# A new order for a fused attention and feed-forward kernel: in-place squares, one ring of eleven tiles, and the last stores in parts

## The chip, the cores and the metric

The kernel runs on one core of a Trainium2 chip. The metric is the device time of one execution in microseconds. The core has five engines that each work through their own list of instructions in order: TensorE (PE, with its weight loads as PEld), VectorE (DVE), ScalarE (ACT), GpSimd (POOL) and SyncE (SP), which here only issues DMAs. An instruction that waits holds up everything behind it on its engine.

## The reference

An attention with a squared relu in place of the softmax, and then a feed-forward block with a quick gelu. There are 8 batches, 12 heads, 448 positions, 64 elements a head; 3584 tokens, 768 model columns and 2048 inner columns.

```python
scores = scale * np.matmul(q, k.transpose(0, 1, 3, 2))
attn = np.maximum(scores, 0.0) ** 2 / S
x = np.matmul(attn, v)          # then the heads side by side: [3584, 768]
h = x @ w_in
g = h * (1.0 / (1.0 + np.exp(-1.702 * h)))
out = g @ w_out
```

The scale and the division by S are left for later in the kernel: the gelu's input and the last copy carry a factor 1/SC.

## The kernel before

**The attention** is cut into 24 units, one for four heads of one batch (three units a batch). A unit has seven blocks j of 64 rows. `scores` (line 150) makes a block's scores with four quarter-array matmuls (64 rows by 64 columns of the array each, side by side) into two PSUM banks. `relu` takes one bank to half of a float16 tile, on VectorE (line 161) or ScalarE (line 163). `square` (line 88 or 169) squares the whole tile on one of three engines into a tile of the pool `at`. `attn_v` (line 182) then multiplies the unit's seven tiles with v, again in quarter-array matmuls, into two banks, and `xt_evac` copies these into the transposed input of the feed-forward block. A relu tile comes from one of three pools `rl0` to `rl2` with one tile each, named by a number in the list; `at` has eight tiles. A square frees the relu tile, attn_v frees the `at` tiles.

**The loads.** k and q come either through GpSimd's queue, which casts them on the way (units 1 to 5, then transposed on TensorE, line 131), or through SP as float32 (`Lk`, `Lq`), are cast on an engine (`K`, `Q`) and are transposed by a DMA from SP (`Rk`, `Rq`, line 119). v comes through GpSimd's queue (`V`, line 104), and so do the weights w_in (eight DMAs, `jwa` and `jwb`, two for each of four blocks) and w_out.

**The feed-forward block** works on eight groups g of 384 and 512 tokens in turn. The first group and part of the second use plain matmuls (`m1`, line 229: `f` in the list). The others use a scheme with seven products of half-size blocks instead of eight (`unit_product`, `u`; sums of blocks are made on VectorE, `S`, `T`, `W`, `A`). Copies out of PSUM (`t`), sums (`b`), the gelu on ScalarE (`g`, line 215) and a widening on GpSimd (`v`, line 218) follow. The second matmul does the same with pairs of token tiles m (`pair_product`, `p`; `h` and `l` take the results to a float32 tile `osb`), and `store` (`o`, line 329) sends each tile out in two DMAs of 64 rows on SP. All full-array matmuls but those of `m1` are recorded at line 204, all two-operand elementwise work at line 88.

**The order** is written out by hand in one long list of words. Each word issues the instructions of one step, in the list's order, to the engine that its suffix names (`:a`, `:d`, `:p`; without one, a home engine), and `@` gives PSUM banks. Every engine thus gets its instructions in the list's order, and between engines only data and free buffers decide. For example `s6.1@0.2 r6.1.1:d@1 x6.1:a` is scores of block 1 of unit 6 into banks 0 and 2, a relu on VectorE into relu pool 1, and the square on ScalarE. Ten matmuls on zeros stand before the list.

Of the kernel before, what the change touches and what calls it, by code (L numbers as in the profile page):

```python
# [9 lines left out]
F16 = mybir.dt.float16  # L10
AF = mybir.ActivationFunctionType
# [4 lines left out]
def kernel(  # L16
# [35 lines left out]
    for name, bufs in (("cst", 1), ("kst", 1), ("qst", 1), ("k16", 2), ("q16", 2), ("v16", 4),  # L52
                       ("kT", 3), ("qT", 3), ("rl0", 1), ("rl1", 1), ("rl2", 1), ("at", 8), ("xe", 1), ("xo", 2),
                       ("T1", 1), ("T2", 1), ("T4", 1), ("ge", 1), ("go", 1), ("gf", 5),
                       ("as0", 1), ("as1", 1), ("osb", 3)):
        pool(name, bufs)
# [97 lines left out]
    rls = {}  # L154

    def relu(e, p, u, j, a):
        if (u, j) not in rls:
            rls[u, j] = new(f"rl{p.pop(0)}", [128, 2, S], F16, "rl")
        o, i = rls[u, j][:, a, :], slots[u, j][a][:, 0:S]
        if e == "d":  # L160
            nc.vector.tensor_scalar(out=o, in0=i, scalar1=0.0, scalar2=None, op0=ALU.max)  # L161
        else:
            nc.scalar.activation(out=o, in_=i, func=AF.Relu)  # L163

    def square(e, p, u, j):
        rl = rls.pop((u, j))
        at = new("at", [128, 2, S], F16)
        if e == "a":
            nc.scalar.activation(out=at, in_=rl, func=AF.Square)  # L169
        else:  # L170
            tt(at, rl, rl, ALU.mult, e)
        slots[u, j] = at
# [157 lines left out]

    def m2(e, p, g, m, h):
        op[g, m, h] = bank(p, "op")
        mm(op[g, m, h][:, 0:NOUT], lambda f: gts[g][:, f, m * 128:(m + 1) * 128],
           lambda f: wout[h][f // WO][:, f % WO, :], NF, True)
# [82 lines left out]
    with tc.manual_schedule():  # L417
# [3 lines left out]
               "l": pair_last, "i": single, "n": m2_out, "jo": load_w_out, "a": attn_v,  # L421
# [27 lines left out]
        zero = new("gf", [128, 1024], F16, "zero")  # L449
        nc.vector.memset(zero[:, 0:512], 0.0)  # L450
        zp = bank([7], "zp")
        for _ in range(10):
            nc.tensor.matmul(out=zp, lhsT=zero[:, 0:128], rhs=zero[:, 0:512],  # L453
                             start=True, stop=True)
        words = (
            "I Lk0 K0:d tk0@0 jk1 Lq0 Q0:a jq1 V1 V0 ek0 tq0@1 jk2 tk1@2 eq0 s0.1@3.4 s0.0@5.6 "
            "ek1 r0.1.1@0 s0.3@7.0 r0.1.0:d r0.3.1@1 tq1@1 r0.3.0:d s0.4@2.4 r0.0.0@2 s0.5@3.0 "
            "x0.1 x0.3 s0.2@7.5 r0.0.1 x0.0 r0.4.0@0 r0.4.1 s0.6@6.2 r0.5.0:d@1 x0.4 r0.6.1@2 eq1 "
            "jq2 tk2@4 s1.0@3.2 r0.5.1 r0.6.0 x0.6 r0.2.1@0 x0.5 r0.2.0 x0.2 ek2 r1.0.0@2 r1.0.1 "
            "x1.0 s1.1@0.6 r1.1.1@1 s1.2@1.5 tq2@7 eq2 r1.2.1:d@0 jwa1 jq3 r1.2.0 jk4 jk3 r1.1.0 "  # L460
            "s1.3@3.2 a0@6.4 jwa0 jwb0 r1.3.1@2 s1.4@1.0 r1.3.0 e0.0.1:a jwb1 x1.3 e0.1.1 jq4 "
            "x1.2:a tq3@7 s1.6@2.5 r1.6.1@2 s2.0@3.4 eq3 e0.0.0 V2 s1.5@7.5 r1.6.0 e0.1.0 "
            "s2.2@6.2 jwa3 r1.4.0:d@0 x1.1:p x1.6 jwb3 r1.4.1 x1.4 tk3@1 ek3 r1.5.1@1 r1.5.0 "
            "r2.0.0@2 tk4@0 r2.0.1 x1.5 s2.3@5.7 r2.3.1@0 s2.1@3.1 r2.3.0 V3 r2.2.0@1 ek4 x2.0 "
            "r2.2.1 r2.1.0@2 a1@4.7 r2.1.1:d x2.3 e1.0.0 s2.5@5.0 r2.5.1:d@0 jq5 e1.0.1:a e1.1.1 "
            "x2.2:a x2.1:p jk5 s2.4@6.2 f0.0.0@1 f0.2.0@3 r2.5.0 f0.2.1 f0.0.1 e1.1.0 s2.6@0.7 "
            "x2.5 s3.0@5.4 r2.4.1@1 f0.3.0@2 r2.4.0 r2.6.0@2 r2.6.1 f0.3.1 jwa2 r3.0.0:d@0 x2.4 "
            "f0.1.0@6 s3.1@0.5 r3.0.1 r3.1.1@1 f0.4.0@7 G3 Lk6 f0.1.1 x2.6 a2@4.5 r3.1.0:d x3.0:p "
            "tq4@0 S1.1 e2.0.0 x3.1 f0.4.1 e2.0.1:a f0.2.2 f0.3.2 e2.1.1 g0.2 jwb2 g0.3 f0.1.2 "
            "e2.1.0:a g0.1 eq4 f0.0.2 s3.4@5.3 s3.3@0.2 r3.4.0:d@2 g0.0 f0.5.0@4 r3.4.1 r3.3.0@0 "  # L470
            "V4 f0.4.2 f0.5.1 g0.4 v0.4 s3.2@6.1 r3.2.1@1 r3.2.0 r3.3.1:d x3.4 x3.3 s3.5@5.3 "
            "s3.6@2.0 f0.5.2 f0.6.0@7 f0.6.1 r3.6.1:d@2 r3.6.0 Lq6 r3.5.0@0 f0.7.0@1 x3.2 r3.5.1 "
            "x3.6 tk5@6 s4.1@0.2 g0.5 s4.0@5.3 r4.1.0@1 v0.1 jo0.1 f0.7.1 f0.7.2 v0.3 f0.6.2 "
            "r4.0.0@2 x3.5 r4.0.1:d ek5 r4.1.1 g0.6 x4.0 v0.5 s4.3@4.0 s4.2@5.3 S0.1 a3@2.6 "
            "r4.3.0@0 s4.4@7.4 g0.7 V5 r4.2.1@2 r4.2.0:d r4.3.1:d tq5@1 e3.0.0:a x4.3 x4.1 "
            "e3.0.1:a x4.2 S0.2 s4.6@3.5 r4.4.0@0 s4.5@0.2 f0.9.0@6 f0.9.1 r4.6.1@1 f0.9.2 eq5 "
            "r4.5.0:d@2 f0.12.0@7 f0.8.0@5 f0.12.1 f0.12.2 r4.6.0:d r4.4.1 f0.10.0@4 f0.10.1 v0.7 "
            "f0.10.2 v0.0 x4.6 r4.5.1 s5.3@2.1 g0.12 g0.9 s5.0@0.7 jo1.0 x4.4:p g0.10 r5.0.0@0 "
            "s5.2@3.6 r5.2.1@1 r5.0.1 x5.0:a f0.8.1 f0.8.2 x4.5 v0.10 r5.3.1:d@2 a4@4.0 e4.0.0:a "
            "s5.6@1.6 v0.12 f0.15.0@7 f0.15.1 f0.15.2 g0.8 r5.3.0:d r5.2.0:d r5.6.1@0 v0.9 S1.2 "  # L480
            "x5.3 r5.6.0:d s5.4@2.3 e4.0.1 s5.1@4.5 g0.15 x5.6:a s5.5@1.6 r5.1.0@2 r5.1.1:d "
            "f0.13.0@0 f0.13.1 f0.13.2 S2.1 S2.2 x5.2:a jo0.0 f0.14.0@7 r5.5.0@0 v0.8 x5.1:p "
            "f0.11.0@5 f0.14.1 f0.14.2 f0.11.1 Q6:d jo1.1 f0.11.2 r5.5.1:d r5.4.1:d@1 r5.4.0 "
            "f1.1.0@4 g0.13 x5.4 f1.5.0@1 v0.2 v0.6 v0.15 f1.1.1 x5.5 f1.5.1 K6:p S2.3 g0.11 "
            "f1.3.0@2 f1.2.0@0 a5@5.6 g0.14 Lk7 e5.0.0:a f1.6.0@3 f1.6.1 f1.0.0@7 e5.0.1:a f1.5.2 "
            "g1.5 S2.4 f1.4.0@5 S3.1 T1.1 T1.2 S3.2 W0.1 v0.14 v0.13 v1.5 f1.4.1 u1.3.0@6 t1.3.0 "
            "f1.1.2 S3.4 Rq6 v0.11 T1.4 g1.1 K7 f1.3.1 f1.4.2 f1.3.2 f1.2.1 f1.2.2 V6 W1.1 W1.2 "
            "W3.1 f1.0.1 f1.0.2 g1.0 u1.2.0@1 t1.2.0 Lq7 u1.3.1@4 v1.1 u1.2.1@7 g1.4 v1.0 b1.2.1 "
            "u1.3.2 Q7:a m0.0.0@5 f1.6.2 g1.2 Rk6 v1.2 b1.3.1 S1.4 W2.1 S0.3 S3.3 Lq8 g1.3 V7 Lk8 "
            "g1.6 Rk7 u1.2.3 v1.4 v1.6 n0.0.0 Rq7 s6.1@0.2 W3.2 s6.0@5.3 r6.0.1@2 W2.2 Q8 "  # L490
            "r6.0.0:d u1.3.3 r6.1.1:d@1 r6.1.0:d u1.2.2 s6.2@3.5 K8:p f1.7.0@2 g1.3.1 v1.3.1 "
            "x6.0:a g1.2.1 r6.2.1:d@0 f1.7.1 f1.7.2 v1.2.1 r6.2.0:d T1.3 t1.3.2 W2.4 t1.2.2 "
            "m0.0.1@0 g1.7 x6.1:a u1.2.4 S1.3 x6.2 s6.4@5.3 n0.0.1:a r6.4.0@2 s6.3@2.0 v1.7 W0.2 "
            "Lq9 t1.2.4:d b1.2.3 v1.3 Rq8 r6.4.1 x6.4 r6.3.1@1 r6.3.0 u1.3.4 t1.3.4:d u1.2.5 "
            "g1.2.5 u1.2.6 Q9 s6.5@5.3 r6.5.1:d@0 s6.6@0.2 x6.3:a b1.2.6 b1.3.3 r6.6.0@2 r6.6.1 "
            "x6.6:a g1.2.6 v1.2.6 m0.1.0@1 Lk9 s7.1@3.0 Rk8 Lq10 s7.0@7.2 r6.5.0:d x6.5 n0.1.0:a "
            "r7.1.0:d@1 r7.0.1@2 K9:p r7.1.1:d r7.0.0 g1.3.3 u1.3.6 b1.3.6 u1.3.5 x7.0 s7.2@5.1 "
            "W3.4 s7.3@3.2 v1.2.5 g1.3.5 r7.2.0@0 r7.2.1 g1.3.6 a6@0.7 g1.2.3 v1.2.3 v1.3.5 "
            "e6.0.1:a s7.4@4.6 r7.3.1:d@2 Lk10 K10:p x7.1 s7.5@5.1 x7.2:a m0.1.1@2 Q10:d e6.0.0 "
            "V11 e6.1.0:a e6.1.1:a r7.4.0@1 r7.3.0:d v1.3.6 r7.4.1 Rq9 r7.5.1@0 r7.5.0:d x7.5:a "  # L500
            "x7.3 x7.4 Rk9 s7.6@0.7 s8.1@3.4 n0.1.1:a r7.6.1@2 s8.0@5.6 r8.0.0:d@1 r7.6.0:d x7.6 "
            "m0.2.0@1 Lq11 r8.1.1:d@0 s8.2@5.2 s8.3@0.7 r8.1.0 o0.1 a7@3.4 r8.0.1 x8.0 r8.3.0@2 "
            "r8.3.1 v1.3.3 A1.0.1@0 r8.2.1@1 V8 V10 Lk11 r8.2.0:d x8.1:a s8.4@6.0 e7.0.0 x8.3 "
            "e7.1.0:a r8.4.0@0 s8.5@7.5 e7.0.1:a Q11 r8.5.0@2 x8.2 A1.0.2@1 r8.4.1 e7.1.1:a "
            "r8.5.1:d x8.5 n0.2.0:a m0.2.1@2 s8.6@3.6 s9.1@7.5 Rk10 r8.6.1@1 x8.4 r9.1.1@2 "
            "s9.0@0.4 r9.0.1@0 p1.0.0@1 n0.2.1:a h1.0.0 r9.0.0 Lq12 s9.3@6.5 r8.6.0:d x8.6 "
            "r9.3.0@1 Rq10 r9.1.0:d W0.3 a8@3.4 s9.2@2.7 r9.3.1 x9.1:a s9.4@0.6 e8.0.1:a K11:d "
            "e8.0.0 W1.3 x9.0 p1.0.2 r9.4.1@2 u2.1.0@5 r9.2.0@0 T2.1 Q12 t2.1.0 T2.2 W1.4 e8.1.1 "
            "u2.0.0@6 u2.1.1@2 b2.1.1 W2.3 T2.3 r9.2.1:d e8.1.0:a t2.0.0 r9.4.0 x9.4:a u2.1.2 "
            "u2.0.2 u2.2.0@3 t2.0.2 u2.0.1@4 g2.1.1 Rq11 t2.1.2 b2.0.1 u2.2.1@0 v2.1.1 g2.0.1 "  # L510
# [154 lines left out]
```

## Time and profile before

| | us |
|---|---|
| median of 13 runs | 373.16 (370.46 to 379.81) |
| profiled execution, device time | 371.45 |
| its span in the trace | 369.7 |
| PE, DVE, ACT, POOL busy | 358.5, 300.6, 269.3, 172.6 |
| mean granted TensorE clock | 0.994 |
| first matmul starts, last one ends | 1.2, 364.1 |

The three ways of squaring a tile take 660 ns on VectorE (97 of them), 952 on ScalarE (49) and 1755 on GpSimd (22); a relu takes 617 ns on VectorE (117) and 555 on ScalarE (219). A group's mean is the time from start to end of one instruction; neighbours on an engine overlap a little, so that a sum of means is some 10% above the busy time. Instructions named `ox` and `hx` are the products of the feed-forward block, `sc` the scores, `av` attn_v.

### The profile page before, as it was taken

How to read it: one execution, taken by the hardware profiler on the slowest of the kernel's cores; microseconds unless marked ns; L12 is line 12 of the kernel's file. 1: busy time of each engine (PE TensorE's matmuls, PEld its weight loads, DVE VectorE, ACT ScalarE, POOL GpSimd, SP SyncE). 2: the span in 40 equal slices, each digit the busy share in tenths (PEclk: the TensorE clock that was granted, in tenths of full speed). 3: DMA queues.
4: the chain of work that ended last, by engine and by line, in shares of the span. 5: the costliest groups of instructions: out<-in, count | busy, mean ns of one | idle time of the engine just before them, and what ended most of it. 6: DMA issues, size and time to landing. Idle time of an engine off the chain costs nothing.

```text
span 369.7 us, 9188 instructions
## 1 busy us (share of the span) xinstructions
PE 358.5 (97%) x3566; PEld 232.5 (63%) x3566; DVE 300.6 (81%) x532; ACT 269.3 (73%) x536; POOL 172.6 (47%) x222
## 2 busy tenths in 40 slices
PE   8899999999899999999999999999999999999993
PEld 4445555655488556875589555885549855688651
DVE  4899999899998887979989888887799689455741
ACT  3897874789798999867777868779978765566311
POOL 6776776736327336475436633146332634115300
PEclk9899999999999999999999999999999999999999
DMA  9999999997995596486953663849073440401224
GB/s 193 189 205 214 237 170 204 200 223 152 190 253 94 122 219 131 111 179 143 189 113 103 140 147 75 181 123 164 12 230 76 70 91 4 111 0 45 78 52 129
DMA packets 64908, 51.39 MB, mean 139 GB/s; under 512 B 35680, under 2 KB 61280, under 8 KB 64864
## 3 DMA queue, kind: packets, MB, share of 16 engines
q1 hardware_dynamic: 48256, 36.71, 42.6%
q0 software_dynamic: 16608, 14.09, 26.5%
q8 instruction: 28, 0.46, 0.5%
q14 instruction: 16, 0.13, 0.1%
HBM read 45.61 MB, written 11.01 MB: 153 GB/s over the span
## 4 chain that ended last, share of the span: by engine, by line
PE 77%; DVE 10%; DMA 4%; issue 3%; ACT 3%; POOL 1%; SPq 0%; DVEq 0%; ACTq 0%; POOLq 0%
PE ox L204 26%; PE hx L204 22%; PE av L182 8%; PE sc L150 7%; PE ht L229 5%; PE os L204 4%; PE op L204 3%; DVE at L88 3%; DVE rl L161 3%; DVE gf L88 2%; DMA q<-in_q_dram 2%; DMA v<-in_v_dram 1%; PE zp L453 1%; DMA out_dram<-osb 1%; ACT rl L163 1%
## 5 line engine op out<-in xcount | busy, mean ns | idle before, releaser
L163 ACT ACTIVATE rl<-sc 128x448 f16<-128x448 f32 x219 | 106.9, 555 | 18.8 <-PE sc L150 13.8
L161 DVE TENSOR_SCALAR rl<-sc 128x448 f16<-128x448 f32 x117 | 69.1, 617 | 8.3 <-PE sc L150 6.9
L218 POOL TENSOR_SCALAR go<-gf 128x512 f16<-128x512 f32 x64 | 43.1, 674 | 62.3 <-ACT gf L215 50.8
L88 DVE TENSOR_TENSOR at<-rl 128x896 f16<-128x896 f16 x97 | 61.8, 660 | 2.3 <-ACT rl L163 0.9
L88 POOL TENSOR_TENSOR at<-rl 128x896 f16<-128x896 f16 x22 | 38.5, 1755 | 50.1 <-ACT rl L163 22.9
L204 PEld LDWEIGHTS <-win 128*128 128x128 f16 x624 | 56.8, 98 | 6.8 <-issue 1.0
L88 DVE TENSOR_TENSOR gf<-hx,gf 128x512 f32<-128x512 f32 (+1 forms) x78 | 47.4, 625 | 15.8 <-PE hx L204 8.3
L218 POOL TENSOR_SCALAR ge<-gf 128x384 f16<-128x384 f32 x64 | 36.6, 572 | 34.6 <-ACT gf L215 31.0
L150 PE MATMUL sc<-qT,kT 64*64 64x448 f16 x672 | 49.9, 359 | 2.3 <-DVE qT L83 1.0
L215 ACT ACTIVATE gf<-gf 128x512 f32<-128x512 f32 (+1 forms) x78 | 43.5, 577 | 7.5 <-DVE gf L88 7.2
L169 ACT ACTIVATE at<-rl 128x896 f16<-128x896 f16 x49 | 46.3, 952 | 2.3 <-DVE rl L161 1.7
L204 PE MATMUL ox<-wout,go 128*128 128x384 f16 x256 | 46.0, 327 | 0.1
L204 PEld LDWEIGHTS <-winS 128*128 128x128 f16 x468 | 42.7, 98 | 5.2 <-issue 1.4
L204 PEld LDWEIGHTS <-go 128*128 128x128 f16 x320 | 30.0, 98 | 24.0 <-issue 5.5
L79 ACT ACTIVATE gf<-hx 128x512 f32<-128x512 f32 (+1 forms) x54 | 28.8, 546 | 16.7 <-PE hx L204 13.7
L204 PEld LDWEIGHTS <-ge 128*128 128x128 f16 x288 | 26.9, 98 | 21.5 <-issue 5.0
L182 PE MATMUL av<-at,v 64*64 64x448 f16 x672 | 37.9, 357 | 0.5 <-DMA v<-in_v_dram 0.4
L204 PE MATMUL hx<-T,winS 128*128 128x256 f16 (+1 forms) x312 | 36.0, 260 | 0.2
L150 PEld LDWEIGHTS <-kT 64*64 64x64 f16 x672 | 18.0, 105 | 24.5 <-issue 18.4
L204 PE MATMUL ox<-wT,asum 128*128 128x384 f16 x176 | 31.6, 327 | 0.0
L204 PE MATMUL hx<-xo,win 128*128 128x256 f16 x252 | 31.4, 273 | 0.1
L182 PEld LDWEIGHTS <-v 64*64 64x64 f16 x672 | 20.9, 109 | 13.6 <-issue 3.6
(78 smaller groups left out, 479.9 us busy)
## 6 DMA issues: line engine op xcount, KB each, us to landing
out_dram<-osb SPq DMA_DIRECT2D x56, 192.0 KB, 3.2
kst<-in_k_dram SPq DMA_DIRECT2D x19, 448.0 KB, 4.7
qst<-in_q_dram SPq DMA_DIRECT2D x19, 448.0 KB, 4.4
v<-in_v_dram POOLq DMA_DIRECT2D x24, 224.0 KB, 6.1
win<-in_moe_w_in_dram POOLq DMA_DIRECT2D x8, 384.0 KB, 10.9
wout<-in_moe_w_out_dram POOLq DMA_DIRECT2D x4, 768.0 KB, 10.3
k<-in_k_dram POOLq DMA_DIRECT2D x5, 224.0 KB, 7.0
q<-in_q_dram POOLq DMA_DIRECT2D x5, 224.0 KB, 7.6
```

The source lines that it names most:

```text
L79: nc.scalar.activation(out=o, in_=i, func=AF.Copy)
L88: eng[e].tensor_tensor(out=o, in0=x, in1=y, op=op)
L150: nc.tensor.matmul(out=sc[a][c, 0:S], lhsT=st["kT"][r, j, c], rhs=st["qT"][r, :, c], start=True, stop=True)
L161: nc.vector.tensor_scalar(out=o, in0=i, scalar1=0.0, scalar2=None, op0=ALU.max)
L163: nc.scalar.activation(out=o, in_=i, func=AF.Relu)
L169: nc.scalar.activation(out=at, in_=rl, func=AF.Square)
L182: nc.tensor.matmul(out=av[s][64 * a:64 * a + 64, 0:S], lhsT=v16[r, a, 64 * j:64 * j + 64], rhs=at[r, a, :], start=(j == 0), stop=(j == J - 1))
L204: nc.tensor.matmul(out=o, lhsT=lhs(i), rhs=rhs(i), start=start and i == 0, stop=i == n - 1, skip_group_check=True)
L215: nc.scalar.activation(out=o, in_=i, func=AF.Gelu_apprx_sigmoid, scale=1.0 / SC)
L218: eng[e].tensor_scalar(out=o, in0=i, scalar1=SC, scalar2=1.0, op0=ALU.mult, op1=ALU.mult)
L229: nc.tensor.matmul(out=hp[g, f][:, 0:n], lhsT=w[:, i, fo:fo + 128], rhs=xts[g][:, i, 0:n], start=i == 0, stop=i == NK - 1)
L453: nc.tensor.matmul(out=zp, lhsT=zero[:, 0:128], rhs=zero[:, 0:512], start=True, stop=True)
```

## The change

The list is a new one. It has the same steps for the same data with 1939 words against 1931, and differs in four ways beside its order.

```diff
-                       ("kT", 3), ("qT", 3), ("rl0", 1), ("rl1", 1), ("rl2", 1), ("at", 8), ("xe", 1), ("xo", 2),
+                       ("kT", 3), ("qT", 3), ("at", 11), ("xe", 1), ("xo", 2),
...
-        if (u, j) not in rls:
-            rls[u, j] = new(f"rl{p.pop(0)}", [128, 2, S], F16, "rl")
+        if (u, j) not in ats:
+            ats[u, j] = new("at", [128, 2, S], F16)
...
     def square(e, p, u, j):
-        rl = rls.pop((u, j))
-        at = new("at", [128, 2, S], F16)
+        at = ats.pop((u, j))
+        slots[u, j] = at
         if e == "a":
-            nc.scalar.activation(out=at, in_=rl, func=AF.Square)
+            nc.scalar.activation(out=at, in_=at, func=AF.Square)
         else:
-            tt(at, rl, rl, ALU.mult, e)
-        slots[u, j] = at
+            tt(at, at, at, ALU.mult, e)
...
+    def store_part(e, p, g, m, h, i):
+        b, j = divmod(gcum[g] + 2 * m + i, J)
+        r0 = b * S + j
+        c = slice(h * NOUT, (h + 1) * NOUT)
+        (nc.scalar if e == "a" else nc.sync).dma_start(
+            out=out[r0:r0 + 63 * J + 1:J, c], in_=osb[g, m][64 * i:64 * i + 64, c])
...
-        zero = new("gf", [128, 1024], F16, "zero")
-        nc.vector.memset(zero[:, 0:512], 0.0)
-        zp = bank([7], "zp")
-        for _ in range(10):
-            nc.tensor.matmul(out=zp, lhsT=zero[:, 0:128], rhs=zero[:, 0:512],
-                             start=True, stop=True)
+        zero = wT[2][:, 0, :]
+        nc.vector.memset(zero, 0.0)
+        zp = []
+
+        def zeros(e, p, n):
+            if p:
+                zp.append(bank(p, "zp"))
+            for _ in range(n):
+                nc.tensor.matmul(out=zp[0][:, 0:NOUT], lhsT=zero[:, 0:128], rhs=zero,
+                                 start=True, stop=True)
+
+        two["z"] = zeros
         words = (
-            "I Lk0 K0:d tk0@0 jk1 Lq0 Q0:a jq1 V1 V0 ek0 tq0@1 jk2 tk1@2 eq0 s0.1@3.4 s0.0@5.6 "
...
+            "Lk0 z13@0 jk1 V1 jq1 I V0 K0:d tk0@1 z1 ek0 jk2 Lq0 Q0:a tq0@2 eq0 tk1@3 s0.3@4.5 "
...
-            "l7.2.1 p7.2.2 A7.2.4 o7.1 p7.2.3 h7.2.2 p7.2.4 p7.0.6 l7.0.6 o7.0 h7.2.4 l7.2.3 "
-            "p7.2.5 l7.2.5:a o7.3 p7.2.6 l7.2.6 o7.2"
+            "q7.2.0.0:a p7.2.3 h7.2.2:d A7.2.4 p7.2.4 o7.1 p7.0.6 h7.2.4:d l7.2.3 l7.0.6 o7.0 "
+            "q7.3.1.1:a q7.2.0.1 q7.3.1.0:a p7.2.5 l7.2.5:a q7.3.0.0 q7.3.0.1 p7.2.6 l7.2.6 "
+            "q7.2.1.1:a q7.2.1.0"
```

The relu writes into the tile that the square then overwrites, so one pool of eleven tiles takes the place of three relu pools and eight tiles. The last two output tiles (7, 2 and 7, 3) go out as eight parts of 64 rows by 384 columns, four on ScalarE's queue and four on SP's, instead of four of 64 rows by 768 columns on SP's. The matmuls on zeros are 14 of 384 columns instead of ten of 512, 13 ahead and one after the first transposes, on a piece of a weight tile. The identity for the transposes is made by GpSimd after its first three loads instead of before them.

How many steps each engine gets, in the two lists:

| step | before: VectorE, ScalarE, GpSimd | after |
|---|---|---|
| relu | 117, 219, 0 | 121, 215, 0 |
| square | 97, 49, 22 | 84, 57, 27 |
| cast of k and q | 10, 8, 20 | 2, 14, 22 |
| copies of half-size products (`t`, `h`) | 37, 74, 0 | 40, 71, 0 |
| last sums and copies (`l`, `n`) | 40, 16, 0 | 41, 15, 0 |

The other steps keep their engines and numbers: 40 of the copies out of attn_v on ScalarE and 32 on VectorE, all gelus on ScalarE, all widenings on GpSimd.

## The prediction

> **What bounds the kernel now.** I read the page's busy times first, then the slices, the stage table, the chain that ended last in order of time, and last the stores at the end.
>
> ```profile
> span 369.7 us, 9188 instructions
> PE 358.5 (97%) x3566; PEld 232.5 (63%) x3566; DVE 300.6 (81%) x532; ACT 269.3 (73%) x536; POOL 172.6 (47%) x222
> PE   8899999999899999999999999999999999999993
> PEclk9899999999999999999999999999999999999999
> ```
>
> TensorE is busy 97% of the span; the next engine, VectorE, 81%. The only weak slices of PE are the first two and the last.
>
> ```profile
> 6.00:16.90 10.90, 9.05 (x146) 5.43 (x144) 10.20 (x19) 8.44 (x19) 7.59 (x11) 0.84 1.22 190
> 30.00:60.00 30.00, 29.84 (x311) 15.76 (x308) 28.67 (x48) 23.32 (x50) 20.42 (x27) 1.00 1.21 211
> 60.00:100.00 40.00, 38.88 (x347) 22.52 (x344) 37.95 (x63) 31.25 (x62) 21.57 (x27) 1.00 1.09 192
> 160.00:260.00 100.00, 99.59 (x1016) 67.52 (x1013) 83.81 (x151) 77.48 (x151) 48.97 (x61) 1.00 0.66 139
> ```
>
> The columns are stretch, length, then PE, PEld, DVE, ACT, POOL busy (with counts), granted clock, DMA share and GB/s. Up to 100 us VectorE is as full as PE (37.95 of 40); later it has 16% to spare. The clock is below 1 only before 17 us.
>
> Busy PE includes matmuls that crawl, so I set the starts of the 3566 matmuls in the timeline against what each kind takes back to back. That comes from the chain: 16 of 384 columns in 2.60 us, six of 256 in 0.64 to 0.66, 28 of attn_v in 1.32. The matmuls without the ten on zeros add up to 325 us. The first matmul starts at 1.2, the last ends at 364.1, so 38 us are something else: 1.2 before the first; 4.3 for the zeros; 12.2 for 111 changes between quarter-array (64x64) and full-array matmuls (below); about 9 for the small steps between groups and the transposes' latency; and about 12 of real waiting beyond each step's median, split into some 5 before 20 us, 1.1 from 20 to 30, and 5.7 from 30 to 364. After the last matmul come 5.6 us. So what an order can still win is small: about ten microseconds inside, two or so at the end.
>
> **The change part by part.**
>
> **In-place squares and one ring: nothing.** There are as many tiles as before (3 and 8 against 11). VectorE's in-place subtraction on go (1024 columns) averages 704 ns, the one from go into asum 776, so in-place costs nothing extra. The ring lets a relu start wherever any tile is free instead of one of three; its worth is in the waits below.
>
> **What moves between engines.** Counted in the two lists, at the page's means. VectorE: 13 squares fewer (x 660 ns, -8.6), eight casts of k and q fewer (4 x 0.65 + 4 x 1.09, -6.9), four relus, three copies out of PSUM, two last sums more and one copy fewer (+5.0): -10.5 us. ScalarE: eight squares (x 952, +7.6) and six casts (+5.7) more, four relus and some copies fewer (-4.3): +9.0. GpSimd: five squares (x 1755) and two casts more: +10.8. With 81, 73 and 47% busy all of it lies beside PE; the cover of VectorE grows just where it was full, up to 100 us. The matmuls are the same ones, and 14 on zeros of 384 columns replace 10 of 512, 5376 columns against 5120; both finish about when k's first cast does (it ends at 4.99), so 0.
>
> **Changes of array mode: +1.3 us.** Here a rule speaks against the change.
>
> ```profile
> 127.60 0.50 PE sc L150 x8
> 128.11 1.41 PE ox L204 x8
> ...
> 201.16 1.30 PE ox L204 x8
> 202.46 1.49 PE hx L204 x18
> ```
>
> Eight ox matmuls between scores hold PE for 1.41 us; between hx products, which are full-array too, 1.30. One change costs 0.11 us; the median over all of them is 0.105 one way and 0.113 the other. The Trainium skill (TensorEngine Tiling (Array Packing), Key Properties) says that changing the tiling mode drains TensorE, but gives no price. In the new list the modes change 138 times against 126, since ten scores stand alone between full-array groups where two did. By the row, 12 x 0.11 = +1.3 us; by the rule, more than nothing. I take the row.
>
> **The start: -0.5 us.** The first load on GpSimd's queue is issued at 1.45 behind the identity; in the new list it comes first, some 0.7 earlier. The loads then land one behind another, 1.1 us apart (k1 6.95, q1 8.11, v1 9.22, v0 10.33, k2 11.46), and PE waits for k2 (11.46, its transposes start at 11.51) and q2 (13.75, at 13.79). Half to all of 0.7 comes through: -0.5. The w_in parts now come in another order. At 1.95 us each behind 1.1 us per k, q or v I get the pairs at about 23, 28, 30 and 40 us, in the order w_in blocks 0, 1, 2, 3; PE wants them at about 25, 32, 33 and 45 (list position plus the 9.6 us by which PE lags its work at 24 us). They are hidden with 2 us left at the least; if that cover is gone, each us late is one us. Bounds -1.5 to +1.5.
>
> **Waits inside: -2.5 us of 5.7.** Two show in the chain.
>
> ```profile
> 94.64 1.20 issue
> 95.84 0.62 DVE rl L161
> 96.46 0.04 issue
> 96.50 0.38 PE sc L150 x3
> ...
> 251.22 5.46 DMA v<-in_v_dram
> 256.73 1.52 PE av L182 x28
> ```
>
> At 95.3 PE waits 1.4 us for a bank that VectorE's relu still holds. At 256 it waits 0.55 for v of unit 18, which GpSimd issued at 251.22, behind widenings. The new list has that load some 60 us of matmul work ahead of its product instead of 4.5, so the 0.55 goes. The other 5.1 are this kind of late reader of a bank, mostly 0.1 to 0.3 each. For every bank that is taken again I added up the matmul work between its last product and the next: under 1.5 us in 32 places before (smallest 0.64) and in 13 in the new list (smallest 1.17), past 25 us. In proportion 5.1 would become 2.1; not every wait is of this kind, so I take -2.0, with 0.55 -2.5. Bounds: -4.5, and 0.
>
> **Late k, q and v: +0.2 us.** The other side of the same list. Matmul work between the later cast of k or q and the unit's first scores: before, 14 us or more from unit 7 to 23; now 7.7 for unit 7, 9.9 for 8, 10.4 for 9, 9.7 and 9.4 for 22 and 23. A cast on GpSimd (1.0 us) and a DMA transpose from issue to landing (7.4 to 8.1 us for units 7 and 8, 3.0 to 5.0 for the late ones) need 9 together around 70 us, and 6 late. SP is in order too: behind a transpose that waits for its cast stand the next loads of k and q and then the stores. Before products, the v of unit 8 has 5.1 us of matmul work and that of unit 6 6.3, against 6.1 median (7.2 to 7.7 there) to land. If GpSimd works exactly at its place in the list, unit 7 is 1.4 late, v of unit 6 0.9, v of unit 8 2.3, unit 9 some 0.5: 5 us is the upper bound, 0 the lower. In the trace of before six such transfers land within 2 us of their use (v of units 2, 8, 14, 18, 23, k of unit 6), and only one made PE wait, 0.55 in all, since an in-order engine that is half idle runs a few us ahead of its place. Six tight ones again: 0.1 each would be 0.5; I take +0.2 because the start now arrives earlier.
>
> **The end: -0.5 us.**
>
> ```profile
> 364.08 0.02 issue
> 364.10 0.56 DVE osb L390
> ...
> 363.00:368.00 5.00, 1.07 (x7) 0.42 (x5) 0.56 (x1) 0.29 (x1) 0.00 (x0) 1.00 0.81 236
> ```
>
> After the last sum (364.66) SP issues two stores of 192 KB one behind the other (median 0.53 each), and the last lands 2.6 us after its issue, at 367.7; the DMA is busy all that time with three tiles (1.18 MB at 236 GB/s). Now only half a tile is left, in two parts of 96 KB, one issued by ScalarE and one by SP; that tile's other half goes before. The Trainium skill (DMA: Bandwidth & Descriptors, Issuing engines are not separate DMA queues) says that issuing from several engines saves only issue time, since all share 16 DMA engines. By it and by the row one issue is saved, 0.5; by half the bytes at 236 GB/s another 0.8 at most, if the backlog sets the end. The latency of 2.6 stays either way, so I take -0.5 (0 to -1.3). ScalarE's DMA issues aren't shown in this trace: at SP's 0.47 to 1.42 two stand ahead of its copy of the second last product, which comes 1.6 us after them; covered up to 0.8 each.
>
> **Sum.** +1.3 - 0.5 - 2.5 + 0.2 - 0.5 = -2.0 us. The profiled execution took 371.45 (span 369.7 and 1.75 around it), so it would take 369.4. The median of the runs, 373.16, stands 0.46% above that execution; 369.4 x 1.0046 = 371.1.
>
> **The rivals.**
>
> *The waits don't shrink (372.8 us).* PE is full already, and some of the 5.7 is the unevenness of the matmuls' own starts, which no order removes. For: outside 95 and 256 us no wait is above 0.3. Against: 32 tight banks become 13. With 0.8 instead of 2.5 and half a us more for late transfers: -2.0 + 1.7 = -0.3, so 372.8.
>
> *Late transposes and v (376 us, slower).* One mechanism, at units 6 to 9, 65 to 105 us: the casts and loads moved towards their use. There DMA is full (share 1.09 in the stage table), VectorE too, and a late kT lets PE run through what full-array work stands in the list and then stop. Price: up to the 5 us above, with -2.0 - 0.2 = -2.2 elsewhere +2.8, so 371.45 + 2.8 times 1.0046 = 375.5; with a cold clock or a second missed bank after it 376 and more. It decides from 3.5 us of such waits on. For: lists of 7.7 us against 9 needed. Against: before, five of six tight transfers cost nothing.
>
> *VectorE or ScalarE becomes the bound.* ScalarE gets 9 us more, 278 of 369, and from unit 0 to 5 it has 40.7 us of back-to-back work against 45.7 of PE's. That is below PE in every stage; I give it no chance of its own.
>
> **How the numbers follow.** Within 0.5% (1.9 us, about what a measurement of this kernel can tell from no change) means 371.3 to 375.0. The likeliest case, 371.1, has 0.50, its own range 368.5 to 372.3; I see 0.42 of it below 371.3. No gain: 0.26, of it 0.03 faster, 0.20 same, 0.03 slower. Late transfers: 0.24, of it 0.21 slower. So faster 0.45, same 0.31, slower 0.24. The range for 8 in 10 goes from the low bounds of waits and end (-4.5 and -1.3, against +1.3: 367.5) to the slow rival, 376.0.
>
> **What would show it.** Right: PE's last matmul ends at 361.5 to 363; no single wait of PE above 1 us past 30 us; VectorE below 292 us busy, ScalarE near 276; the last landing 3.2 us after the last matmul instead of 3.7. Wrong: PE idle before scores with the transposes of units 7 to 9 as releaser, or before attn_v of units 6 or 8 with v's DMA; PE waiting for w_in at 24 to 46 us; or the same end of PE with the same small waits. I would be most wrong if a late unit 7 delayed relus, squares and widenings behind it as well.

## The result, and the profile after

| | before | after |
|---|---|---|
| median of the runs, us | 373.39 (48 runs, 370.46 to 379.81) | 369.21 (11 runs, 368.68 to 371.75) |
| ratio of the times | | 0.9898 (95% interval 0.9870 to 0.9925) |
| profiled execution, device time and span | 371.45, 369.7 | 371.75, 369.9 |
| PE, DVE, ACT, POOL busy | 358.5, 300.6, 269.3, 172.6 | 358.2, 289.0, 276.6, 178.5 |

The kernel became 1.0% faster, 4.2 us between the medians; 2.0 were forecast. The ratio and its interval leave out a few runs of before that fell into a slower state, so the ratio is not quite the quotient of the two medians.

The two profiled executions are the wrong pair to compare. That of before is one of its better ones (371.45 against a median of 373.4); that of after is the slowest of its eleven. A common execution of the new order is at hand from the experiment `e4_tail_balanced` below, the new kernel with one of its eight last stores on another queue and the same time (368.97): its profiled execution took 368.84, with a span of 367.1. Where I say "the common execution" I mean this one.

The page of after, its busy times and the rows of PE in the slices:

```profile
span 369.9 us, 9086 instructions
PE 358.2 (97%) x3570; PEld 231.4 (63%) x3570; DVE 289.0 (78%) x519; ACT 276.6 (75%) x542; POOL 178.5 (48%) x229
PE   6979999999999999999999999999999999999994
PEclk9899999999999999999999999999999999999999
```

Between the second slice and the last PE shows a 9 in all but one; that one (7) lies at 18 to 28 us. VectorE is 11.6 us less busy and ScalarE 7.3 more, as the two lists said. Now the stage table of after, with the columns of the table of before (stretch, length, PE, PEld, DVE, ACT, POOL busy, clock, DMA share, GB/s):

```profile
6.00:16.90 10.90, 8.20 (x119) 4.35 (x121) 7.61 (x14) 6.81 (x16) 6.59 (x8) 0.84 1.20 183
30.00:60.00 30.00, 30.00 (x322) 15.03 (x315) 25.64 (x45) 25.12 (x51) 21.82 (x26) 1.00 1.26 216
60.00:100.00 40.00, 39.33 (x336) 23.39 (x333) 34.02 (x58) 29.93 (x58) 23.36 (x30) 1.00 0.85 174
160.00:260.00 100.00, 99.58 (x1025) 68.26 (x1026) 79.45 (x143) 84.69 (x161) 54.19 (x67) 1.00 0.60 139
```

and the common execution, the same first and third stretch:

```profile
6.00:16.90 10.90, 9.90 (x171) 5.50 (x165) 10.38 (x18) 9.09 (x22) 8.61 (x11) 1.00 1.25 198
60.00:100.00 40.00, 39.34 (x345) 23.18 (x344) 34.06 (x59) 31.83 (x62) 22.41 (x28) 1.00 0.87 168
```

From 60 to 100 us VectorE was at 37.95 of 40 before and is at 34 now, and the DMA share went from 1.09 to 0.85 and 0.87: the two resources that were full there have room. The first stretch is where the two executions of the new order part: 8.20 against 9.90 us of PE, with a clock of 0.84 and 1.00.

What PE waited for, as the trace sums it up (engine, operation and line, what it waited for; total, times, longest): first after, then the common execution.

```profile
PE tr L131 <- DMA k<-in_k_dram: 1.8, 1, 1.8
PE zp L463 <- DVE wT L456: 1.2, 1, 1.2
PE ht L228 <- DMA win<-in_moe_w_in_dram: 1.0, 1, 1.0
PE tr L131 <- DMA q<-in_q_dram: 0.9, 2, 0.6
...
```

```profile
PE zp L463 <- DVE wT L456: 1.2, 1, 1.2
PE sc L150 <- DVE at L161: 0.6, 2, 0.3
PE tr L131 <- DMA q<-in_q_dram: 0.4, 1, 0.4
...
```

The second line is the wait for the memset ahead of the matmuls on zeros, which every trace has. The other long waits of after are all before 30 us, for loads; in neither execution does PE wait for a DMA past 30 us. Before waited for v at 256 us, and in two other traces of its order for v of unit 8 too (below).

To compare stages I use one reading throughout. The list of a kernel gives the matmul work that stands ahead of any matmul, counted back to back, changes of array mode included. Subtract it from the time at which that matmul starts in the trace, and what is left is the lag: everything that PE lost up to there.

| lag in us, at | before | its order, three more traces | after | common execution |
|---|---|---|---|---|
| attn_v of unit 5 | 9.8 | 9.9, 10.1, 9.7 | 11.0 | 8.0 |
| end of the last matmul | 14.0 | 16.4, 17.1, 15.5 | 14.0 | 11.0 |
| between the two | 4.2 | 6.5, 7.0, 5.8 | 3.0 | 3.0 |
| from last matmul to the end of the span | 5.6 | 4.7 (parts), 5.8, 5.7 | 4.7 | 4.8 |

The three more traces are those of `e1_tail_parts`, `e2_v_early` and `e3_ring`, which keep the order of before but for the last stores, six loads, or the squares in place. So the common execution of the new order against these four: the start -1.9, the waits inside -2.9 (5.9 in the mean against 3.0), the end -0.9, and the list itself 1.2 longer by its twelve more mode changes. That sums to -4.5, against -4.2 between the medians.

### The profile page after: what moved, and what is told of

It reads as the page before. It is cut to its first block, busy times and chain, and to the rows that moved or that the text cites. A ratio compares the mean times of both kernels' runs of the same rounds, so it can differ in the third digit from the quotient of the medians.

```text
span 369.9 us, 9086 instructions
## 1 busy us (share of the span) xinstructions
PE 358.2 (97%) x3570; PEld 231.4 (63%) x3570; DVE 289.0 (78%) x519; ACT 276.6 (75%) x542; POOL 178.5 (48%) x229
## 4 chain that ended last, share of the span: by engine, by line
PE 85%; DVE 6%; DMA 4%; POOL 1%; ACT 1%; issue 1%; POOLq 0%; DVEq 0%
PE hx L203 29%; PE ox L203 26%; PE sc L150 9%; PE ht L228 7%; PE av L181 7%; PE os L203 4%; PE op L203 3%; DMA win<-in_moe_w_in_dram 2%; DMA k<-in_k_dram 2%; DVE at L161 2%; DVE wT L88 1%; DVE at L88 1%; ACT at L163 1%; DVE asum L88 1%; PE tr L131 1%
## 5 line engine op out<-in xcount | busy, mean ns | idle before, releaser
L163 ACT ACTIVATE at<-sc 128x448 f16<-128x448 f32 x215 | 105.2, 571 | 16.2 <-PE sc L150 15.7
L161 DVE TENSOR_SCALAR at<-sc 128x448 f16<-128x448 f32 x121 | 71.9, 617 | 13.2 <-PE sc L150 12.7
L217 POOL TENSOR_SCALAR go<-gf 128x512 f16<-128x512 f32 x64 | 41.2, 644 | 63.8 <-ACT gf L214 47.0
L88 POOL TENSOR_TENSOR at<-at 128x896 f16<-128x896 f16 x27 | 45.6, 1693 | 29.9 <-ACT at L163 18.8
L169 ACT ACTIVATE at<-at 128x896 f16<-128x896 f16 x57 | 53.9, 956 | 0.9 <-DVE at L161 0.6
L150 PE MATMUL sc<-qT,kT 64*64 64x448 f16 x672 | 52.7, 365 | 1.3 <-DVE at L161 0.6
L88 DVE TENSOR_TENSOR at<-at 128x896 f16<-128x896 f16 x84 | 51.4, 646 | 1.0 <-ACT at L163 0.6
L203 PEld LDWEIGHTS <-go 128*128 128x128 f16 x320 | 29.8, 98 | 22.7 <-issue 4.8
L79 ACT ACTIVATE gf<-hx 128x512 f32<-128x512 f32 (+1 forms) x51 | 27.2, 543 | 15.3 <-PE hx L203 7.2
L181 PE MATMUL av<-at,v 64*64 64x448 f16 x672 | 36.1, 350 | 0.1
L150 PEld LDWEIGHTS <-kT 64*64 64x64 f16 x672 | 17.7, 106 | 26.8 <-issue 21.9
L203 PEld LDWEIGHTS <-asum 128*128 128x128 f16 x200 | 18.6, 98 | 15.3 <-issue 3.1
## 6 DMA issues: line engine op xcount, KB each, us to landing
wout<-in_moe_w_out_dram POOLq DMA_DIRECT2D x4, 768.0 KB, 11.6
```

Source lines behind the costliest of these rows:

```text
L79: nc.scalar.activation(out=o, in_=i, func=AF.Copy)
L88: eng[e].tensor_tensor(out=o, in0=x, in1=y, op=op)
L150: nc.tensor.matmul(out=sc[a][c, 0:S], lhsT=st["kT"][r, j, c], rhs=st["qT"][r, :, c], start=True, stop=True)
L169: nc.scalar.activation(out=at, in_=at, func=AF.Square)
L181: nc.tensor.matmul(out=av[s][64 * a:64 * a + 64, 0:S], lhsT=v16[r, a, 64 * j:64 * j + 64], rhs=at[r, a, :], start=(j == 0), stop=(j == J - 1))
L203: nc.tensor.matmul(out=o, lhsT=lhs(i), rhs=rhs(i), start=start and i == 0, stop=i == n - 1, skip_group_check=True)
```

## The experiments

All were timed in five rounds beside runs of the kernel before on the same chip: 373.42 (29 runs) beside the first four, 373.24 (17 runs) beside the others. The suffix of a word in the list is its engine, as above.

### The last two tiles in parts, alone

```diff
 # list of before, its last words
-... l7.2.1 p7.2.2 ... l7.2.3 p7.2.5 l7.2.5:a o7.3 p7.2.6 l7.2.6 o7.2
+... l7.2.1 q7.2.0.0:a p7.2.2 ... l7.2.3 q7.3.1.1:a q7.2.0.1 q7.3.1.0:a p7.2.5 l7.2.5:a
+q7.3.0.0 q7.3.0.1 p7.2.6 l7.2.6 q7.2.1.1:a q7.2.1.0
```

> The kernel before, its order untouched, with only its last two tiles stored in the eight parts of the change. The prediction's step for the end: 0.5 us less than before (0 to 1.3), so a ratio of 0.9987. Rival, that the end is not set by the last tile's bytes but by SP, which still issues six DMAs one behind the other: 0 to 0.5 us slower, ratio 1.000 to 1.001, the last DMA on SP issued more than 0.5 us after the last sum.

Measured: 372.06 (12 runs), ratio 0.9974 (0.9934 to 1.0013). The time alone doesn't settle it; the trace does. From the end of the last matmul to the end of the span it takes 4.7 us; 5.6, 5.8 and 5.7 with the stores whole. All ten traces agree: 4.6 to 4.8 in the five with parts, 5.5 to 5.8 in the five without.

Its waits show what the profiled execution of before had been spared:

```profile
PE av L182 <- DMA v<-in_v_dram: 1.6, 2, 1.2
PE zp L460 <- DVE zero L457: 1.2, 1, 1.2
```

1.2 us of the 1.6 is v of unit 8 at 102 us, the rest v of unit 18 at 258. In the trace of before only the second was seen.

### The loads of v earlier, alone

```diff
 # list of before: V8, V13, V14, V15, V18 and V23 moved up by 15 to 20 us of matmul work, e.g.
-... r8.2.1@1 V8 V10 ...
+... m0.0.1@0 V8 g1.7 ... r8.2.1@1 V10 ...
```

> The kernel before with six loads of v (units 8, 13, 14, 15, 18, 23) moved some 15 to 20 us of matmul work ahead in the list, nothing else. If loads that land just in time are what makes PE wait in the kernel before, and vary from execution to execution, the median falls by 1 to 2 us (ratio 0.995 to 0.997) and the highest times come down. If PE's waits for late PSUM readers are the larger part, as the prediction's step has it, 0.5 us less (0.9985).

Measured: 374.66 (12 runs), ratio 1.0025 (0.9988 to 1.0063): nothing gained. The waits for v are gone from the trace, and another took their place. The chain of waits of this kernel, 157 to 167 us (start, length, what):

```profile
157.68 5.43 DMA qst<-in_q_dram
...
163.27 0.91 POOL q L83
164.18 0.71 POOL v L104
164.89 0.08 issue
164.97 0.62 POOL go L218
165.59 0.02 issue
165.61 0.61 ACT gf L79
166.22 0.02 issue
166.24 0.70 DVE gf L88
166.94 0.04 issue
166.99 0.27 PE hx L204
```

GpSimd waits for a load of q to cast it; behind the cast stands one of the moved loads of v (unit 14, 0.71 us to issue) and behind that the widening that frees a gf tile. ScalarE's copy, VectorE's sum and then PE wait for it: PE 1.8 us for that gf. So here an early v was not free: it was paid by a widening that it was moved ahead of. That the new list has its loads of v early and few such waits is therefore not the effect of these six moves alone.

### Squares in place and the ring, alone

```diff
-                       ("kT", 3), ("qT", 3), ("rl0", 1), ("rl1", 1), ("rl2", 1), ("at", 8), ...
+                       ("kT", 3), ("qT", 3), ("at", 11), ...
...
-            rls[u, j] = new(f"rl{p.pop(0)}", [128, 2, S], F16, "rl")
+            rls[u, j] = new("at", [128, 2, S], F16)
...
-        at = new("at", [128, 2, S], F16)
+        at = rl
```

> The kernel before with the squares in place and one pool of eleven tiles, in its own order. The prediction: nothing by itself (within 0.3 us, ratio 0.999 to 1.001). Rival, that relus were held up by the three relu tiles: 1 us or more faster (ratio 0.997 or less), with ScalarE's and VectorE's waits for a square gone.

Measured: 373.43 (12 runs), ratio 0.9988 (0.9956 to 1.0021). Nothing, as the sum had it. The rival's sign came, its gain did not: of ScalarE's waits for a square before,

```profile
ACT rl L163 <- DVE at L88: 2.9, 4, 1.2
ACT rl L163 <- POOL at L88: 1.2, 1, 1.2
```

none is left in this trace, and the time is the same. In this order they lay beside PE.

### The parts spread evenly over two queues

```diff
 # list of after
-... l7.2.5:a q7.3.0.0 q7.3.0.1 p7.2.6 ...
+... l7.2.5:a q7.3.0.0:a q7.3.0.1 p7.2.6 ...
```

> The changed kernel with one of its eight last parts (the first half of tile 7,3's first half-columns) issued by ScalarE instead of SP. If SP's queue sets the end of the changed kernel, the last issue on SP comes 0.6 us earlier and the kernel is 0.5 us faster than the changed kernel's 369.2 (368.7); if the DMA engines or the latency set it, the same as the changed kernel. Its profile is also a second look at the changed order: if the start of the first profile (first k by GpSimd's queue landing at 8.8 us) was one slow execution, this one has it near 7 us and its last matmul ends at 362 to 363 us instead of 364.9.

Measured: 368.97 (6 runs, 368.84 to 371.27), ratio to before 0.9882 (0.9837 to 0.9927): the same as the new kernel. In it SP issues its last store 0.78 us after the last matmul instead of 1.45, and the span still ends 4.83 us after that matmul, where after had 4.72. So the last issue on SP does not set the end.

### Work taken off VectorE, alone

```diff
 # list of before: 13 squares and the casts of k and q on other engines, no word moved, e.g.
-... x4.3 x4.1 e3.0.1:a x4.2 S0.2 ... S1.2 x5.3 r5.6.0:d ... p4.0.3 K21:d u5.2.5 ...
+... x4.3 x4.1:a e3.0.1:a x4.2:a S0.2 ... S1.2 x5.3:p r5.6.0:d ... p4.0.3 K21 u5.2.5 ...
```

> The order of before with 13 squares taken off VectorE (eight to ScalarE, five to GpSimd, in units 4 to 18) and the casts of k and q on the engines of the new list; nothing else is moved. My theory (the list's distances between a bank's uses decide the waits, the engines' loads lie beside PE): as before, 372.5 to 374.5, with VectorE near 289 us busy and the same waits of PE. Rival (a VectorE that is too full holds the banks): the waits past 30 us fall from about 6 to 2.5 us, and the time to 369.5 to 370.5.

Measured: 385.94 (6 runs), ratio 1.0310 (1.0253 to 1.0368). Both theories missed it: the shift neither lies beside PE nor helps, it costs 12.7 us. (Of the 14 casts that change their engine, eight leave VectorE; six go from ScalarE to GpSimd or back, as in the new list.) One place shows how. Chain of waits, 256 to 272 us:

```profile
256.52 0.62 ACT gf L215
257.14 0.85 ACT k L79
257.99 0.02 issue
258.01 3.67 DMA kst<-in_k_dram
...
261.76 0.13 ACT k L79
261.88 0.73 issue
262.61 0.62 ACT gf L215
...
264.31 0.62 POOL go L218
...
265.69 5.62 DMA v<-in_v_dram
271.31 0.04 issue
271.35 0.75 PE av L182 x9
```

A cast of k frees the staging buffer at 258, the next load is issued, and the cast that needs it (unit 21, on VectorE before) now waits at the head of ScalarE's queue until 261.7. The gelus behind it are late, so are GpSimd's widenings, and so is the load of v behind these, at 265.69; attn_v of unit 18 waits. PE lost 0.8 us here directly. It loses time in many places of this trace (the lag from attn_v of unit 5 to the end is 14.6 us against 4.2), but this is the only one followed back to a cast; how the 12.7 us divide between the casts and the squares is not shown. A busy share of 73% says nothing of what a wait costs at the head of that engine's queue. The new list gives each engine the same number of squares and casts (84, 57 and 27 squares; 2, 14 and 22 casts) without these waits, so the numbers alone don't make them. My choice of the 13 squares is not the new list's; that another choice costs less was not tried.

A rival is left open. Here each of the three relu pools still has one tile, and a square on ScalarE (952 ns) or GpSimd (1755) keeps it longer than one on VectorE (660). The first of the two lines under `e3_ring` reads in this trace

```profile
ACT rl L163 <- DVE at L88: 4.3, 7, 1.2
```

and with the other engines' squares the relus of ScalarE and VectorE wait 6.7 us for a square, against 4.1 before and none in `e3_ring`. The shift together with the ring of eleven tiles was not run, so part of the 12.7 us may belong to the pools.

### The heads of the two lists exchanged

```diff
 # first: words 1 to 150 of the new list, then what remains of the list of before, in its order
+Lk0 z13@0 jk1 V1 jq1 I V0 ... V3 f0.2.1 f0.0.0@1 f0.0.1 | jwa3 jwb3 f0.1.0@6 r3.0.1 s3.1@0.7 ...
 # second: words 1 to 145 of the list of before, then what remains of the new list
+z13@7 I Lk0 K0:d tk0@0 jk1 ... jwa2 r3.0.0:d x2.4 | jwb2 tq4@6 eq4 ... s3.1@0.7 ...
```

At the seam a few PSUM banks have other numbers, so that no step takes a bank that a later one still reads.

> The new list's first 150 words (up to attn_v of unit 1 and the scores of unit 2), then all other words in the order of before; squares in place, ring of 11, stores whole. My theory (the start gives 1.7 us by its order alone): attn_v of unit 2 at 26.5 to 27.0 instead of 28.5, and 371.3 to 372.2 in all. Rival (what is won at the start is lost at the next late transfer, or it is one execution's luck): 373 to 374.

> The other way round: the first 145 words of before, then the new list's other words, its stores in parts too. My theory: 1.7 us worse than the new list, 370.5 to 371.5, with the waits past 30 us as few as there (about 2.3 us). Rival: 369 to 369.6, if the start gives nothing in the end; above 372 if the new list's later order needs its early start (late v or transposes at units 6 to 9).

Measured: new head before the old rest 375.35 (12 runs), ratio 1.0039 (1.0010 to 1.0067); old head before the new rest 379.87 (6 runs), 1.0168 (1.0128 to 1.0207). Neither gives what was expected of the start (with the new head, attn_v of unit 2 starts at 30.3 us instead of 26.5 to 27.0), and the waits of PE tell why: new head, then old head.

```profile
PE ht L228 <- DMA win<-in_moe_w_in_dram: 1.1, 1, 1.1
```

```profile
PE ht L228 <- DMA win<-in_moe_w_in_dram: 6.6, 1, 6.6
```

A head loads the blocks of w_in in the order in which its own rest uses them. The new list begins with products of block 0 and soon takes block 2; the old head loads block 3 before block 2, and PE stands 6.6 us from 33.9 on for a part that was issued at 27.1 and landed at 40.3. With the new head the chain of waits holds a part of w_in from 17.7 to 29.4 us, ahead of attn_v of unit 2. So these two runs don't measure the start. What they do show is the part behind it. Lag from attn_v of unit 5 to the end: 4.6 with the old rest behind the new head, 3.5 with the new rest behind the old one. The waits inside follow the rest of the list, not its head: 4.2 to 7.0 in the five traces with the old rest, 3.0 to 3.5 in the three with the new one. One reservation: behind the old head the new rest starts some 9 us late, which may give its loads more time.

### More mode changes

```diff
 # list of after, in 26 places of units 6 to 23, e.g.
-... s11.6@5.0 s11.2@6.1 p1.2.6 r11.6.0:d ...
+... s11.6@5.0 p1.2.6 s11.2@6.1 r11.6.0:d ...
```

> The new list with the last scores of 26 groups (units 6 to 23) put behind the next full-array step, so that PE changes its array mode 190 times instead of 138. At the row's 0.11 us: +5.7, so 374.5 to 375.5, without new waits of PE. Rival (a change is mostly hidden, the 0.11 is the scores' own pace): below 372. Rival (the later scores make new waits for relus): above 377, seen as waits of PE with a relu as releaser.

Measured: 380.71 (6 runs), ratio to before 1.0182 (1.0145 to 1.0220); 11.5 us more than the new list, twice the 5.7. The third expectation came true, and the price of 0.11 was too low as well. Past 30 us the 172 changes took 20.6 us without their waits, against 13.3 for 119 in the common execution: 0.14 for each added one, not 0.11, since scores that stand alone pay more (0.129 into full-array work at the median instead of 0.105). The waits beyond the medians came to 7.1 us against 2.6. The largest, in the chain of waits:

```profile
225.59 2.17 DVE go L88
227.76 0.55 DVE at L161
228.31 0.04 issue
228.35 0.38 PE sc L150 x4
```

A relu that comes with the later scores stands on VectorE behind a long subtraction on go (2.17 us), and the next scores wait 1.3 us for its bank. So steps that PE takes up to 1.4 us later brought 4.5 us of waits on top of 7.3 of changes.

## Why the prediction was right, and where it fell short

The forecast was 371.1 us, faster; measured were 369.2, inside the wide range of 367.5 to 376.0, and the sign was right. The gain was twice the forecast. By its steps:

- **In-place squares and the ring, 0.** Right: 0.9988 alone. A square on VectorE took 646 ns in place (660 before).
- **Engines, 0.** Right in the sum, wrong in its reason. In the new list VectorE and ScalarE came out as forecast (289.0 and 276.6 busy), and no step waits for them longer than 0.7 us past 30 us. But "all of it lies beside PE" was argued from busy shares, and the same numbers of squares and casts with the words left in the old places cost 12.7 us (with relu pools of one tile, see above). An idle share is no cover by itself. Less work on VectorE did not make the waits fewer there; whether it helps in the new list is not shown.
- **Mode changes, +1.3.** Right for this list: outside waits a change takes 0.112 us in after, 12 of them 1.3. The price is not a constant, as 0.14 for added single scores shows.
- **Waits inside, -2.5, and late transfers, +0.2.** Right in size: 2.9 less in the mean of four traces, both sides of the late-transfer step included. The make-up is another matter. The forecast put 0.55 us of it down to v and 2.0 to banks still being read; in PE's waits, v stands for 0.4 us in before, 1.6 in `e1_tail_parts`, 1.4 in `e3_ring` and nothing in the new order, so that late loads of v were a larger part than forecast and the banks at most the rest. No transfer was late in the new order past 30 us. The loads of v for units 6 and 8, feared most, landed 3.3 and 3.0 us ahead of their products, and the transposes of units 7 to 9 took 3.6 to 6.3 us instead of the 7.4 to 8.1 taken from before for units 7 and 8 (k of unit 8 took 5.7 there), while the DMA share from 60 to 100 us fell to 0.85. That GpSimd works near its place in the list was right (v of unit 6 was issued 0.9 us behind it); that a load then takes 6 to 7.7 us was not (3.7). What I under-rated was the gap to before: its profiled execution has 4.2 us of such losses, three others of its order 5.8 to 7.0. The forecast scaled one good execution by 0.46%.
- **The start, -0.5.** The term that was mis-sized. The first load was issued only 0.2 us earlier (1.25 instead of 1.45), not 0.7, and it landed at 6.3 in the common execution and at 8.8 in after's own, against 6.9 to 7.5 in four traces of before. So attn_v of unit 2 starts at 26.6 or 29.8 (28.2 in the trace with more mode changes, which has the same head), against 28.4 to 28.6. What a common execution gains there follows from the medians, by subtraction: -4.2 less the other three terms (-2.9, -0.9, +1.2) leaves -1.6. The traces alone don't show it: 26.6, 29.8 and 28.2 are 28.2 in the mean, 0.3 below before's. In the common execution the chain from 8 to 30 us holds no load; VectorE and ScalarE are on it for most of the time, both busy 10.00 of 10.00 us from 15 to 25, where they had 8.85 and 8.92 before and the chain held a load of q for 6.1 us. How much of the gain belongs to the order of the loads and how much to the engines I could not part, because the exchanged heads failed on w_in. The step on w_in itself held for the common execution: the four pairs landed at 23.4, 28.6, 30.6 and 42.0 us against 23, 28, 30 and 40, and PE waited for none.
- **The end, -0.5.** Mis-sized too: -0.9. The last landing came 0.3 us sooner after the last matmul (3.7 to 3.9 instead of 4.0 to 4.2), a little less than forecast. The rest, some 0.6, is the stretch from the last landing to the end of the span, 1.6 us with the stores whole (1.3 in one trace of five) and 1.0 in parts. I had no term for it, and what happens in it is not shown.

Of the signs named in advance: last matmul at 361.5 to 363 came in the common execution (362.2), not in after's (365.2); no wait of PE above 1 us past 30 held in both; VectorE and ScalarE fit. The last landing came 3.7 to 3.9 us after the last matmul, not 3.2. One sign of being wrong came in after's own execution: PE waited 1.0 us for w_in, up to 27.1 us. The rival with late transfers at units 6 to 9 fell with the margins above. The rival in which the waits don't shrink fell with 3.0 against 4.2 to 7.0.

Some of the forecast's working does not come out. Before's last store landed at 368.1 us, 4.0 after the last matmul, not at 367.7. The rival in which the waits don't shrink left out its own half us and is 373.4, not 372.8; the slow rival, 371.45 + 2.8 times 1.0046, is 376.0, not 375.5; and the low end of the range, by the terms it names, is 368.6, not 367.5. The result lies inside either range.

Not tried, and so open: the shift of work together with the ring, the new list with its last stores whole, with other PSUM bank numbers, with its loads of v as late as before, and the old head with the blocks of w_in in the new list's order. In particular the step from "13 tight banks instead of 32" to "fewer waits" is argued, not shown: the waits follow the rest of the list, but nothing here parts the banks from its other properties.

## What to carry to other kernels

Take the stages' losses from several executions before a sum is scaled from one: here one profile had 4.2 us of waits where its siblings had 6. Price a moved step by what waits behind it on its engine, not by the engine's busy share: 13 squares and 14 casts given to ScalarE (busy 73%) and GpSimd (47%) cost 12.7 us, and six early loads gained nothing, one of them holding up a widening for which PE then waited 1.8 us. And treat the order of loads and the order of their use as one thing: exchanged heads of two lists that each work well cost up to 6.6 us at one late block.

## What the runs showed of the hardware that was not expected

The same code starts differently from execution to execution. From issue to landing the first load on GpSimd's queue took 5.1 to 5.2 us in three traces of the new head and 7.6 in the fourth, and 5.5 to 7.5 in six with the old one; the next ones land behind it one by one, so the whole start shifts.

The granted clock at the start varies too. A stretch of before and the same of the common execution:

```profile
13.50:16.90 3.40, 3.10 (x38) 1.90 (x42) 3.30 (x7) 2.94 (x7) 2.96 (x5) 0.50 1.21 188
```

```profile
13.50:16.90 3.40, 3.28 (x67) 2.02 (x66) 3.40 (x7) 3.40 (x9) 2.02 (x3) 1.00 1.23 190
```

Before had the clock halved for 3.4 us after PE had had little to do (1.35 and 1.05 us of 2 from 10 to 14 us), and after's own execution at 8.4 to 11.8 us, behind 0.68 of 2 from 6 to 8. The Trainium skill (TensorE: Matmul & The Clock Gate, Part 1: The HAM clock gate) says that the clock has two states and that the activity of a window of 3.4 us decides; the stretches here have that length and that half. That PE's activity decides is not shown here. From 10 to 14 us PE was as busy in `e2_v_early`, whose clock was then halved at 13.6, as in `e3_ring`, which kept the full one:

```profile
10.00:14.00 4.00, 2.42 (x42) 1.04 (x34) 4.00 (x9) 3.79 (x9) 1.76 (x3) 0.94 1.22 186
```

```profile
10.00:14.00 4.00, 2.42 (x42) 1.09 (x42) 3.88 (x9) 3.52 (x9) 1.70 (x3) 1.00 1.24 202
```

Nor did the half clock set the pace of the start in this pair: `e3_ring` had it nowhere from 4 us to the last matmul and reached attn_v of unit 2 at 28.6, before at 28.4. Over 46 runs of before, the 13 with a mean clock under 0.9915 have a median of 375.2 us and the other 33 one of 372.9; of the new kernel and its evenly stored variant, 1 of 18 was as low. Whether the clock is cause or sign of a late load there, these runs don't tell.
